# Two attention blocks on one core: the softmax sums of a turn fetched by two transfers of two rows, and another seed for the planner

## The chip, the cores and the metric

The kernel runs on one core of a Trainium2 chip. The metric is the time of one execution in microseconds on the device; the time of a version is the median of several runs. A separate execution is taken with the hardware profiler, and all lines of a profile come from that one execution. The engines are named as in the profile: PE (TensorE, matmuls), ACT (ScalarE, activations), DVE (VectorE), POOL (GpSimd) and SP (SyncE, which here only issues transfers). A transfer (DMA) issued by SP goes through SP's own in-order queue: an issue that has to wait holds those behind it.

## The reference

Input `x` has 2048 tokens of 1024 features in bf16; there are 32 heads of 32 features. Four residual blocks follow each other, A, B, A, B, each on a layer-normalised input:

- Block A is linear attention. With `q`, `k`, `v = x @ wqkv`, both `q` and `k` are mapped to `concat(softmax(w_phi q), softmax(-w_phi q))` per head; then `kv = sum_s phi_k v`, `z = sum_s phi_k`, and `o = (phi_q kv) / (phi_q z + 1e-6)`.
- Block B is full softmax attention: `p = softmax(q k^T / sqrt(32))`, `o = p v`.

Each ends with `x = x + o @ wo`. The change touches block B alone: the division of the weighted values by the sums of the softmax.

## The kernel before

The program is built in two rounds ("layers" in the code); a round is a block A and a block B. Tokens are cut into 4 chunks of 512, features into 8 groups of 128 (4 heads each). `xT` holds the residual stream transposed and stays in SBUF.

Every piece of work is first declared as an operation with an engine, a guessed duration, dependencies, buffers and a due number (`prio`). `Sched.run` (from line 170) then plays a list scheduler in the building program: on every engine it takes the ready operation with the smallest due number for which buffers are free, and the order in which operations are taken is the order in which the instructions are written. [...] Buffers are limited by class (`QUOTA`, line 329: four of `T`, two of `cden`, two of `den`, and so on), so the guessed times also set when buffers are thought to come free.

Two details of the scheduler belong to the change. First, at the head of `run` every planned duration of a DVE or PE operation is multiplied by a random factor between 0.99 and 1.01, drawn in order of declaration from a generator seeded with `TIE` (line 56). Transfers take no draw. The factors alter the plan, not the instructions themselves:

```
draw = random.Random(TIE)
for o in self.ops:
    if TIE and o.eng in ("DVE", "PE"):
        o.dur *= 1 + draw.uniform(-0.01, 0.01)
```

Second, a transfer is declared by `dma` (line 520) with 0.55 us of issue time on its queue and a latency of `2.0 + kb / 200` us, to which `slack` is added; `kb` also lengthens a common model of the transfer engines (`ring`) by `kb / 400` us.

Block B is `attention` (line 1211). It runs over turns, pairs of a query chunk `qc` and a head group `g`; there are 32 turns in a round. A turn has two halves `pp` of two heads each. For every unit of 128 keys and one head PE computes scores (line 1257) into PSUM; ACT exponentiates two or three units at once (line 1273), and some units go to DVE instead, with a polynomial of five instructions (lines 1184 to 1203). PE then multiplies the exponentials with the values and with ones (line 1305), so the accumulator of a half holds, in one 64-partition half, the weighted values of two heads, and in the other half their sums, each sum repeated over 32 partitions. Which half is which alternates with `pp`. In the gaps PE does "filler" work of the same round or of the next one: projections of keys, queries and values, output projections, and in the first round the key side of the next block A.

When a half is done, DVE copies the accumulator to an SBUF tile `T` (line 1321). When both are, a turn is finished as follows (lines 1351 to 1373):

1. The four sum rows of the turn's four heads, 512 float32 each, are fetched by transfers on SP's queue out of the two `T` tiles and spread over the 128 partitions of `cden`: 32 partitions of 16 numbers for each head (line 1354). The transfers out of a `T` tile need only that tile's copy.
2. DVE takes the reciprocal of `cden`, 128 x 16 (line 1361).
3. SP writes it to a DRAM scratch tensor `rd`, 8 KB (line 1362), and fetches it back with each head's row repeated over 32 partitions, 128 x 512 float32, into `den` (line 1364).
4. DVE multiplies the two `T` tiles with it (line 1370) and leaves the turn's output in bf16 for the output projection.

The last turn of a round divides in another way (lines 1328 to 1349), so 62 of the 64 turns do this. SP's queue also carries the pieces of the keys (line 1049), the swapped halves of the queries (lines 1070 and 1071), queries put away and fetched back in the first round (lines 1083, 1091 to 1093) and the stores of the result (line 1172). Loads of weights in the attention go over POOL's queue (lines 705 and 709).

Of the kernel before, what the change touches and what calls it, by code (L numbers as in the profile page):

```python
# [52 lines left out]
OVER = {"DVE": 0.085, "ACT": 0.012}  # L53
NEXT = {"DVE": 0.05, "ACT": 0.13}
RING = 0.5
TIE = 17
LOOK = 8


# [10 lines left out]
class Sched:  # L70
# [11 lines left out]
    def op(self, eng, dur, fn, deps=(), bufs=(), prio=0.0, lat=None, mode=None):  # L82
        o = Op(eng, dur, LAT[eng] if lat is None else lat, fn, tuple(bufs), prio, mode, len(self.ops))
        for d in deps:
            if d is not None:
                d.out.append(o)
                o.ndep += 1
        for b in o.bufs:
            b.left += 1
        if eng == "DVE" and any(b.kind == "ps" and b.banks in ([(7,)], [(6,)]) for b in o.bufs):  # L90
            o.ahead = EVAC
        self.ops.append(o)
        return o
# [76 lines left out]
    def run(self):  # L170
# [4 lines that stand above are left out]
# [201 lines left out]
def kernel(  # L376
# [11 lines left out]
    nc = tc.nc  # L388
# [47 lines left out]
    for j in range(4):  # L436
# [4 lines left out]
        out=rep[:].rearrange("p (x j) -> p x j", j=4),  # L441
        in_=J_bf[:].rearrange("p (j d) -> p d j", d=32)[:, 0:8, :],
    )
    nc.vector.tensor_copy(out=fold[:], in_=ident[:, 0:32])
    for a in range(1, 4):
        nc.vector.tensor_tensor(
            out=fold[:], in0=fold[:], in1=ident[:, 32 * a:32 * a + 32], op=ALU.add
# [4 lines left out]
        out=selb[:].rearrange("p (j d) -> p j d", d=32),  # L452
        in_=pick[:].unsqueeze(2).to_broadcast([P, 4, 32]),
# [32 lines left out]
    def sb(cls, *dims, dt=BF16):  # L486
        n = 1
        for d in dims:
            n *= d
        b = Buf("sb", -(-n * (4 if dt == F32 else 2) // 64) * 64, cls)  # L490
        b.with_ = ()

        def v():
            ap = arena[:, b.at // 2:b.at // 2 + n * (2 if dt == F32 else 1)]
            if dt == F32:
                ap = ap.bitcast(F32)
            if len(dims) == 2:
                ap = ap.rearrange("p (a b) -> p a b", a=dims[0])
            elif len(dims) == 3:
                ap = ap.rearrange("p (a b c) -> p a b c", a=dims[0], b=dims[1])  # L500
            return ap

        return b, v
# [16 lines left out]
    def dma(prio, fn, deps=(), bufs=(), q="SP", kb=256, issue=0.55):  # L520
        return op(q, issue, fn, deps, bufs, prio, lat=2.0 + kb / 200.0)
# [202 lines left out]
    def phi():  # L724
        return phi_t[:].rearrange("p (g n) -> p g n", g=G)
# [485 lines left out]
    def attention(base, kT, vT, q_of, gate, extra):  # L1211


        def when(u):
            return base + 10 * pos[(u[0], u[1])] + 5 * u[2] + 0.5 * u[3]
# [12 lines left out]
        while units:  # L1228
# [17 lines left out]
            prio = front = max(front, when(grp[0]))  # L1246
# [19 lines left out]
            if own is not None:  # L1266
# [7 lines left out]
                out=e_v(), in_=s_v()[:, 0:w * C512], func=ACT.Exp, scale=math.log(2) / BITS),  # L1274
# [6 lines left out]
        if True:  # L1281
            for qc, g in turns:
                T = []
                end = (qc, g) == turns[-1]
                for pp in range(2):
# [5 lines left out]
                    for n, (d, u) in enumerate(order):  # L1291
                        prio = base + 10 * pos[(qc, g)] + 5 * pp + 0.5 * (n // 2)
# [31 lines left out]
                prio = base + 10 * pos[(qc, g)] + 12  # L1324
# [3 lines left out]
                if end:  # L1328
# [3 lines left out]
                        out=r_v()[hi_, b * P:(b + 1) * P], in_=T[0][1]()[hi_, b * P:(b + 1) * P]),  # L1332
                        [T[0][2]], [d_b, T[0][0]], prio) for b in range(4)]
                    s = [op("DVE", dve_us(512), lambda o_v=o_v, r_v=r_v, T=T: nc.vector.tensor_tensor(
                        out=o_v()[lo_, :], in0=T[0][1]()[lo_, :], in1=r_v()[hi_, :], op=ALU.mult),
# [3 lines left out]
                    for ns in (slice(0, 256), slice(256, 512)):  # L1339
                        ln = op("ACT", act_us(256), lambda ns=ns, l_v=l_v, a_v=a_v: nc.scalar.activation(  # L1340
                            out=l_v()[lo_, ns], in_=a_v()[lo_, ns], func=ACT.Ln), [last], [a_b, l_b], prio)
                        ln = op("ACT", act_us(256), lambda ns=ns, l_v=l_v: nc.scalar.activation(
                            out=l_v()[lo_, ns], in_=l_v()[lo_, ns], func=ACT.Exp, scale=-1.0), [ln], [l_b], prio)
                        cut.append(s + [op("DVE", dve_us(256), lambda ns=ns, o_v=o_v, l_v=l_v, a_v=a_v: nc.vector.tensor_tensor(
                            out=o_v()[hi_, ns], in0=a_v()[hi_, ns], in1=l_v()[lo_, ns], op=ALU.mult),
# [5 lines left out]
                c_b, c_v = sb("cden", 16, dt=F32)  # L1351
                at_d = rd_v[len(gone)]
                gone.append((qc, g))
                m = [dma(prio, lambda k=k, i=i, c_v=c_v, T=T: nc.sync.dma_start(
                    out=c_v()[64 * k + 32 * i:64 * k + 32 * i + 32, :],
                    in_=T[k][1]()[64 * (1 - k) + 32 * i:64 * (1 - k) + 32 * i + 1, :].rearrange(
                        "r (s c) -> r s c", c=16)),
                    [T[k][2]], [c_b, T[k][0]], kb=2) for k in range(2) for i in range(2)]
                for o in m:
                    o.slack = 1.5  # L1360
                rc = op("DVE", 0.245, lambda c_v=c_v: nc.vector.reciprocal(out=c_v(), in_=c_v()), m, [c_b], prio)
# [1 line left out]
                    out=at_d.rearrange("h (s c) -> (h s) c", c=16), in_=c_v()), [rc], [c_b], kb=8)  # L1363
                bk = dma(prio, lambda r_v=r_v, at_d=at_d: nc.sync.dma_start(
                    out=r_v(), in_=at_d.unsqueeze(1).to_broadcast([4, 32, C512])), [aw], [d_b], kb=600)
# [3 lines left out]
                for k, a in ((1, slice(0, P)), (0, lo_)):  # L1369
                    s.append(op("DVE", dve_us(512), lambda a=a, k=k, o_v=o_v, r_v=r_v, T=T: nc.vector.tensor_tensor(  # L1370
                        out=o_v()[a, :], in0=T[k][1]()[a, :], in1=r_v()[a, :], op=ALU.mult),
# [9 lines left out]
        out=phi()[32 * j:32 * j + 32, :, 32 * j:32 * j + 32],  # L1381
        in_=A_w_phi.rearrange("(g j) i f -> j i g f", j=4)[j]), (), (), q="GQ", kb=16) for j in range(4)]
# [14 lines left out]
    for layer in range(2):  # L1397
# [29 lines left out]
        else:  # L1427
            wq_s = [slab("slab", second - 15 + fc, wdq_v[:, :, fc * C512:(fc + 1) * C512], C512, [store["q"][fc]])
                    for fc in range(2)]
            for c in range(NC - 1):  # L1430
                x_b, x_v = sb("xn", PO, C512)
                xnA[c] = (x_b, x_v, [dma(second - 20 + 20 * c + 0.001 * i, lambda c=c, x_v=x_v, i=i: nc.gpsimd.dma_start(
                    out=x_v()[:, 2 * i:2 * i + 2, :], in_=xd_v[:, c, 2 * i:2 * i + 2, :]),
# [53 lines left out]
        if wide == NC:  # L1487
            for i in range(pos[(2, HALF)], len(turns)):
                qc, g = turns[i]
                pl = at + 10 * i - LATE  # L1490
                wl = slab("w2", pl - 3, B_w[:, :, g * P:(g + 1) * P], P, [q_of[turns[i - 2]][2][0]])
                q_of[(qc, g)] = b_q(g, qc, pl, wl, FIL)
        oTs, last_s = attention(at, kT, vT, q_of, gate, lambda i: PAIRS[COUNT[layer][i]])
        if last:
            bo_s = [slab("slab", at + BO + fc, B_o[:, :, fc * C512:(fc + 1) * C512], C512, [q_of[(1, G - 1)][2][0]])
# [42 lines left out]
        if not last:  # L1538

            kv = new_kv()  # L1540
            for c, p0 in AK:
# [4 lines left out]
                    out=xd_v[:, c, 2 * i:2 * i + 2, :], in_=xv()[:, 2 * i:2 * i + 2, :]), [fin[i]], [xb], q="GQ", kb=256)  # L1546
# [46 lines left out]
```

## Time and profile before

| | us |
|---|---|
| runs, median of 3 | 2245.67 (2244.37 to 2248.56) |
| profiled execution | 2247.36 |
| its span, first to last instruction | 2245.1 |
| PE busy in the span | 2176.1 |
| ACT busy | 1985.7 |
| DVE busy | 1855.9 |
| POOL busy | 197.0 |
| line 1273, exponentials on ACT, 1366 instructions | 1668.5 |
| line 1361, reciprocals on DVE, 62 instructions | 15.0 |
| line 1370, multiplies on DVE, 124 instructions | 83.9 |

How to read the lines: `L1273` is line 1273 of the kernel; `arena` is the one large SBUF tile in which the scheduler places nearly all buffers, so most names in a line are `arena`, `psum` or a DRAM tensor. `out<-in` gives what an instruction writes and reads. A row of the busy shares has 40 digits, one for each fortieth of the span, in tenths. A row of a table by stretches of time gives, for each engine, busy microseconds and in brackets the number of instructions, then the clock granted to PE, the share of the DMA engines' time and the rate in GB/s. A row of waits gives who waited, for what, total microseconds, how often, and the longest. A row in order of time gives the start, the duration, engine and line, the operation, and in square brackets the idle time before it with what ended it; `SPq` is an issue on SP's queue, whose duration is that of issuing, not that of the data's way. Consecutive instructions of one line are merged (`x2`). A row for a line of the source gives minimum, median and maximum duration in ns, and the first and last start.

PE and ACT instructions overlap a little with their neighbours, so a busy share near 100% is not yet a full engine.

### The profile page before, as it was taken

The page shows a single profiled execution, that of the slowest core. Times are in us where ns is not written, and L with a number is a line of the kernel's source. Part 1 is how long each engine was busy: PE and PEld are TensorE (multiplying, and loading weights), DVE is VectorE, ACT ScalarE, POOL GpSimd, SP SyncE. Part 2 cuts the span into 40 slices and gives each one's busy share as a digit, 9 for nine tenths or more (in the row PEclk, how much of TensorE's full clock was granted, in tenths as well). Part 3 has the DMA queues.
Part 4 walks back from the last instruction along what each step waited for, and adds up shares of the span by engine and source line. Part 5 has one row for each costly group of instructions (what it writes and reads, how often), then busy time and mean ns, then how long its engine had stood idle before and what let it go on. Part 6 is the DMA issues. An engine that isn't in the chain of part 4 may idle for free.

```text
span 2245.1 us, 82636 instructions
## 1 busy us (share of the span) xinstructions
PE 2176.1 (97%) x36788; PEld 872.2 (39%) x36788; DVE 1855.9 (83%) x2761; ACT 1985.7 (88%) x1939; POOL 197.0 (9%) x299
## 2 busy tenths in 40 slices
PE   7999999999999999999999999999999999999999
PEld 4554454444333333333333444433333333333333
DVE  7986873698899889677887788799999999988968
ACT  4436669999999999999998555999999999999998
POOL 1110000000001010121124200000000000100000
PEclk9999999999999999999999999999999999999999
DMA  9220101111122221222235100111111100211111
GB/s 207 49 81 3 33 24 42 41 34 34 51 57 88 74 73 54 64 96 73 78 110 152 59 5 10 36 37 38 36 29 29 35 24 19 73 31 35 47 36 38
DMA packets 121789, 119.67 MB, mean 53 GB/s; under 512 B 57752, under 2 KB 99800, under 8 KB 121432
## 3 DMA queue, kind: packets, MB, share of 16 engines
q1 hardware_dynamic: 102392, 56.64, 10.0%
q0 software_dynamic: 17424, 56.18, 8.7%
q8 instruction: 287, 4.70, 0.9%
q10 hardware_dynamic: 1616, 1.57, 0.2%
q14 instruction: 70, 0.57, 0.1%
HBM read 79.23 MB, written 14.14 MB: 42 GB/s over the span
## 4 chain that ended last, share of the span: by engine, by line
PE 28%; ACT 23%; DVE 9%; issue 5%; DMA 1%; SPq 0%; ACTq 0%; DVEq 0%
ACT arena L1273 22%; PE psum L530 14%; PE psum L1305 6%; PE psum L1257 6%; DVE arena L1203 2%; DVE arena L1184 1%; DVE arena L1196 1%; DVE arena L1201 1%; DVE arena L1193 1%; ACT arena L823 1%; DMA arena<-arena 1%; DVE arena L1370 1%; DVE arena L1198 1%; DVE arena L1057 1%; PE psum L994 0%
## 5 line engine op out<-in xcount | busy, mean ns | idle before, releaser
L1273 ACT ACTIVATE arena<-psum 128x1536 bf16<-128x1536 f32 (+1 forms) x1366 | 1668.5, 1446 | 12.0 <-PE psum L1257 7.1
L530 PE MATMUL psum<-arena 128*32 128x512 bf16 (+1 forms) x18432 | 1058.3, 358 | 12.5 <-DVE arena L836 2.7
L530 PEld LDWEIGHTS <-arena 128*32 128x32 bf16 x18944 | 459.8, 96 | 447.2 <-issue 175.7
L1305 PE MATMUL psum<-arena 128*32 128x512 bf16 x4096 | 628.1, 383 | 4.0 <-issue 2.0
L1305 PE MATMUL psum<-arena,ones_bf 128*32 128x512 bf16 x4096 | 628.1, 383 | 0.0
L1257 PE MATMUL psum<-arena 32*128 32x512 bf16 x4096 | 536.2, 383 | 27.2 <-ACT arena L1273 22.4
L1257 PEld LDWEIGHTS <-arena 32*128 32x128 bf16 x4096 | 158.4, 91 | 555.8 <-issue 549.0
L1184 DVE TENSOR_SCALAR arena<-psum 128x512 int32<-128x512 f32 x418 | 284.5, 686 | 101.7 <-PE psum L1257 90.3
L1203 DVE SCALAR_TENSOR_TENSOR arena<-arena 128x1024 int16<-128x1024 int32 x209 | 254.7, 1218 | 5.7 <-DVE arena L1201 0.4
L1305 PEld LDWEIGHTS <-arena 128*32 128x32 bf16 x4096 | 163.2, 95 | 227.8 <-issue 177.0
L1305 PEld LDWEIGHTS <-ones_bf 128*32 128x32 bf16 x4096 | 161.3, 95 | 22.3 <-issue 7.9
L705 POOL DMA_DIRECT2D arena<-in_B_wqkv_dram x46 | 42.2, 919 | 1248.6 <-PE psum L530 302.5
L1193 DVE TENSOR_SCALAR arena<-arena 128x1024 f16<-128x1024 int16 x209 | 143.8, 690 | 4.4 <-DMA arena<-arena 0.3
L1196 DVE TENSOR_TENSOR arena<-arena 128x1024 f16<-128x1024 f16 x209 | 142.6, 684 | 4.6
L1201 DVE TENSOR_TENSOR arena<-arena 128x1024 f16<-128x1024 f16 x209 | 142.6, 684 | 3.1
L1057 DVE CAST arena<-psum 128x512 bf16<-128x512 f32 x128 | 87.7, 685 | 57.6 <-PE psum L530 57.3
L823 ACT ACTIVATE arena<-psum 128x512 bf16<-128x512 f32 x80 | 43.0, 596 | 82.6 <-PE psum L530 66.7
L827 DVE TENSOR_REDUCE arena<-arena 128x32 f32<-128x1024 bf16 x64 | 77.0, 1214 | 33.3 <-ACT arena L823 33.2
L530 PE MATMUL psum<-xT,onesD 128*32 128x512 bf16 x1144 | 103.1, 381 | 1.3 <-DVE arena L836 0.7
L1321 DVE COPY arena<-psum 128x512 f32<-128x512 f32 x126 | 86.3, 685 | 15.4 <-PE psum L1305 15.0
L1198 DVE TENSOR_SCALAR arena<-arena 128x1024 f16<-128x1024 f16 x209 | 87.9, 422 | 1.7
L836 DVE TENSOR_TENSOR arena<-psum,arena 128x1024 bf16<-128x1024 f32 x64 | 77.4, 1219 | 13.3 <-PE psum L530 9.7
(124 smaller groups left out, 1383.6 us busy)
## 6 DMA issues: line engine op xcount, KB each, us to landing
arena<-rd SPq DMA_DIRECT2D x62, 256.0 KB
arena<-in_B_wqkv_dram POOLq DMA_DIRECT2D x58, 256.0 KB, 4.1
arena<-in_B_wo_dram POOLq DMA_DIRECT2D x40, 256.0 KB, 4.4
arena<-arena SPq DMA_DIRECT2D x256, 32.0 KB
arena<-wd_k POOLq DMA_DIRECT2D x32, 256.0 KB, 5.0
arena<-in_A_wqkv_dram POOLq DMA_DIRECT2D x32, 256.0 KB, 4.6
arena<-arena SPq DMA_DIRECT2D x96, 64.0 KB
arena<-arena SPq DMA_DIRECT2D x248, 2.0 KB
```

The source lines that it names most:

```text
L530: nc.tensor.matmul(out_[ks, :], lhsT=lhsT[:, ks], rhs=rhs, start=start, stop=stop, tile_position=(0, 32 * k), skip_group_check=True)
L1057: return op("DVE", dve_us(512), lambda: nc.vector.tensor_copy(out=dst(), in_=src()), [dep], bufs, prio)
L1184: o = op("DVE", dve_us(512), lambda: nc.vector.tensor_scalar(out=x_v()[:, k, :].bitcast(I32), in0=s_v()[:, x * C512:(x + 1) * C512], scala ...
L1193: last = op("DVE", 1024 / 1920 + 0.15, lambda: nc.vector.tensor_scalar(out=z(), in0=x_v().bitcast(I16).rearrange("p a (n two) -> p a n two ...
L1196: last = op("DVE", 1024 / 1920 + 0.15, lambda: nc.vector.tensor_tensor(out=u(), in0=z(), in1=z(), op=ALU.mult), [last], [z_b, u_b], prio + ...
L1198: last = op("DVE", 1024 / 3840 + 0.15, lambda: nc.vector.tensor_scalar(out=u(), in0=u(), scalar1=POW2_C[0], scalar2=POW2_C[1], op0=ALU.mul ...
L1201: last = op("DVE", 1024 / 1920 + 0.15, lambda: nc.vector.tensor_tensor(out=u(), in0=z(), in1=u(), op=ALU.mult), [last], [z_b, u_b], prio + ...
L1203: return op("DVE", dve_us(1024), lambda: nc.vector.scalar_tensor_tensor(out=y_v().bitcast(I16), in0=x_v().bitcast(I32), scalar=128.0 / BIT ...
L1257: nc.tensor.matmul(out=s_v()[:, x * C512:(x + 1) * C512], lhsT=kT[g][1]()[r, pp, d * P:(d + 1) * P], rhs=q_of[(qc, g)][1]()[r, (pp + j // ...
L1273: ex = op("ACT", act_us(w * C512), lambda s_v=s_v, e_v=e_v, w=w: nc.scalar.activation(out=e_v(), in_=s_v()[:, 0:w * C512], func=ACT.Exp, s ...
L1305: nc.tensor.matmul(out=a_v()[col:col + 32, :], lhsT=v_v()[:, kc % 4, o:o + DH] if what == 0 else ones_bf[:], rhs=ev()[:, x * C512:(x + 1) ...
L1321: cp = op("DVE", dve_us(512), lambda t_v=t_v, a_v=a_v: nc.vector.tensor_copy(out=t_v(), in_=a_v()), [last], [a_b, t_b], prio - 4)
```

## The change

Line 1354 declared four transfers for a turn: for each `T` tile `k` and each head `i` of it, one row of 512 numbers into 32 partitions. Now there are two: for each `T` tile one transfer whose source is the two rows 32 partitions apart, and whose target is 64 partitions. The declared size is 4 KB instead of 2 for each. The reciprocal depends on two transfers instead of four. The slack of 1.5 us is the same. Besides, the seed `TIE` goes from 17 to 19.

```
-TIE = 17
+TIE = 19
...
-                m = [dma(prio, lambda k=k, i=i, c_v=c_v, T=T: nc.sync.dma_start(
-                    out=c_v()[64 * k + 32 * i:64 * k + 32 * i + 32, :],
-                    in_=T[k][1]()[64 * (1 - k) + 32 * i:64 * (1 - k) + 32 * i + 1, :].rearrange(
+                m = [dma(prio, lambda k=k, c_v=c_v, T=T: nc.sync.dma_start(
+                    out=c_v()[64 * k:64 * k + 64, :],
+                    in_=T[k][1]()[64 * (1 - k):64 * (1 - k) + 33:32, :].rearrange(
                         "r (s c) -> r s c", c=16)),
-                    [T[k][2]], [c_b, T[k][0]], kb=2) for k in range(2) for i in range(2)]
+                    [T[k][2]], [c_b, T[k][0]], kb=4) for k in range(2)]
```

## The prediction

> **What bounds the kernel now.** I read the page first (span, busy shares, the chain that ended last), then the busy time by stage, then the waits of each engine and of the DMA queue, and last the instructions of single turns in order of time. From the page:
>
> ```profile
> span 2245.1 us, 82636 instructions
> PE 2176.1 (97%) x36788; PEld 872.2 (39%) x36788; DVE 1855.9 (83%) x2761; ACT 1985.7 (88%) x1939; POOL 197.0 (9%) x299
> ...
> ACT  4436669999999999999998555999999999999998
> ...
> PE 28%; ACT 23%; DVE 9%; issue 5%; DMA 1%; SPq 0%; ACTq 0%; DVEq 0%
> ACT arena L1273 22%; PE psum L530 14%; PE psum L1305 6%; PE psum L1257 6%; DVE arena L1203 2%; DVE arena L1184 1%; DVE arena L1196 1%; DVE arena L1201 1%; DVE arena L1193 1%; ACT arena L823 1%; DMA arena<-arena 1%; DVE arena L1370 1%; DVE arena L1198 1%; DVE arena L1057 1%; PE psum L994 0%
> ```
>
> The ACT row shows two long runs of nines: the attention of the first and of the second round. There the exponentials of line 1273 hold the chain; outside them it is TensorE. DMA is 1% of the chain, SyncE's queue 0%. I cut the span at the edges of those runs:
>
> ```profile
> core 0: us, PE busy (x) PEld busy (x) DVE busy (x) ACT busy (x) POOL busy (x), PEclk, DMA share, GB/s
> 0.00:327.00 327.00, 306.55 (x6839) 163.46 (x6843) 263.27 (x367) 172.01 (x291) 31.35 (x66) 1.00 0.30 67
> 327.00:1187.00 860.00, 838.02 (x13337) 309.10 (x13330) 675.21 (x997) 851.50 (x726) 109.82 (x153) 1.00 0.23 65
> 1187.00:1440.00 253.00, 248.71 (x4788) 117.92 (x4776) 196.72 (x277) 167.34 (x254) 34.46 (x56) 0.99 0.19 52
> 1440.00:2235.00 795.00, 776.76 (x11711) 278.64 (x11709) 716.28 (x1114) 792.50 (x665) 21.38 (x25) 1.00 0.13 35
> ```
>
> In the first attention ScalarE is idle 860.0 - 851.5 = 8.5 us, in the second 795.0 - 792.5 = 2.5 us. Between them TensorE is idle 253.0 - 248.7 = 4.3 us. These are what a better order could win; for what a worse one could lose the rows give no such limit.
>
> **The change, part by part.** It edits two things: the transfers of line 1354, and the seed TIE. One turn's path through line 1354 on SyncE's queue and VectorE:
>
> ```profile
> 1014.22 1.17 SPq L1354 DMA_DIRECT2D arena<-arena  x2
> 1019.77 0.33 SPq L1362 DMA_DIRECT2D rd<-arena  x1
> 1022.16 0.58 SPq L1364 DMA_DIRECT2D arena<-rd  x1
> ```
>
> ```profile
> 1019.49 0.25 DVE L1361 RECIPROCAL arena<-arena 128x16 f32<-128x16 f32 x1
> ...
> 1031.83 0.68 DVE L1370 TENSOR_TENSOR arena<-arena 128x512 bf16<-128x512 f32 x1
> ```
>
> The second pair of one-row transfers goes out at 1014.22, the reciprocal starts at 1019.49, its result goes to DRAM at 1019.77 and is fetched back at 1022.16, and the first multiply starts at 1031.83, among other VectorE work. The queue holds nothing between these times; it waits.
>
> *Transfers removed.* The queue's row for line 1354:
>
> ```profile
> L1354 SPq DMA_DIRECT2D arena<-arena x248: 502/582/1520, 349.1 to 2215.2; - x124
> ```
>
> 248 one-row issues are 62 turns x 4. The change leaves 124, so at 0.582 us each SyncE's queue is free of 124 x 0.582 = 72 us, if an issue of two rows costs what one of one row does; if it costs what two cost (1.17 us, above) nothing is freed. The bytes are the same. What this frees on the path is bounded by what waits for DMA:
>
> ```profile
> DVE arena L1065 <- DMA arena<-rd: 3.2, 1, 3.2
> DVE arena L1361 <- DMA qd<-arena: 1.0, 1, 1.0
> DVE arena L1370 <- DMA arena<-rd: 0.6, 1, 0.6
> DVE arena L1361 <- DMA arena<-arena: 0.5, 2, 0.3
> DVE arena L1193 <- DMA arena<-arena: 0.3, 1, 0.3
> ```
>
> ```profile
> SPq L1354 <- DVE arena L1321: 288.4, 85, 19.0
> ```
>
> VectorE waits for transfers 3.2 + 1.0 + 0.6 + 0.5 + 0.3 = 5.6 us in all (the wait for the input at the start apart), and the queue itself stands 288 us at line 1354 waiting for the copy of the sums. So the 72 us come out of slack. One place is different, early in the second attention, where the key transfers of line 1049 fill the queue:
>
> ```profile
> 1510.38 0.59 SPq L1364 DMA_DIRECT2D arena<-rd  x1
> ...
> 1512.88 1.23 SPq L1354 DMA_DIRECT2D arena<-arena  x2
> 1514.21 8.31 SPq L1049 DMA_DIRECT2D arena<-arena  x8
> ```
>
> ```profile
> 1510.38 7.76 DMA arena<-rd
> ```
>
> ```profile
> 1518.23 0.69 DVE L1370 TENSOR_TENSOR arena<-arena 128x512 bf16<-128x512 f32 x1 [0.59 <-DMA arena<-rd]
> ```
>
> Eight issues take 8.31 us there, over a microsecond each, and the fetch issued at 1510.38 lands only 7.76 us later. Fewer issues ahead of it are worth that 0.6 us. I take -0.6; the ends are 0 and -5.6.
>
> *Landing of a two-row transfer.* No row shows one. The reciprocal at line 1361 needs both transfers. In the planner each issue is 0.55 us, so the pair that closes a turn is promised 0.55 us sooner and the reciprocal's place in VectorE's order moves up by as much. Now it starts 1019.49 - 1014.22 = 5.3 us after the first issue of the pair; then it is some 4.7 us. It is queued on VectorE in order, so a late landing holds every VectorE instruction behind it, the evacuations of line 1184 among them, and through these ScalarE and TensorE. Against that, the 128-piece transfer of line 1362 lets its successor go 1022.16 - 1019.77 = 2.4 us after its own issue, landing included. So 2.3 us of margin remain. The ends are 0 and the case of a transfer that lands after 4.7 us (a rival below). Line 1361 now waits 1.0 + 0.5 = 1.5 us in 3 of 62 turns; with 0.55 us less margin I take as much again, +1.5.
>
> *Moved work.* The write-back of line 1362, the fetch of line 1364 and the two multiplies of line 1370 may each be placed up to about 0.55 us sooner. Between 1022.16 and 1031.83 lie 9.7 us, and the tiles T, cden and den have at least two buffers. I cost this at nothing; what covers it is that gap, and if it were gone the multiplies would hold VectorE as line 1361 does. SyncE's other work (key pieces, query swaps, stores) moves up in the queue at most by the 1.2 us that a turn saves. GpSimd's queue gets and loses no issue.
>
> *The other seed.* TIE sets the random factors of 0.99 to 1.01 on each planned VectorE and TensorE duration, which decide ties. Every factor changes, so the whole written order changes, from the start of the kernel on. No row prices this; the spread between stretches of the present order is the nearest:
>
> ```profile
> core 0: us, ACT busy (x), PEclk, DMA share, GB/s
> ...
> 700.00:800.00 100.00, 100.00 (x84) 1.00 0.28 79
> 800.00:900.00 100.00, 99.82 (x86) 1.00 0.22 61
> 900.00:1000.00 100.00, 97.03 (x86) 0.98 0.26 79
> 1000.00:1100.00 100.00, 99.25 (x88) 1.00 0.29 82
> 1100.00:1187.00 87.00, 83.92 (x77) 0.98 0.32 103
> ...
> 1800.00:1900.00 100.00, 100.00 (x86) 1.00 0.09 23
> 1900.00:2000.00 100.00, 100.00 (x86) 1.00 0.19 53
> ```
>
> Stretches lose between 0.0 and 3.1 us of ScalarE. In the stretches of 3.0 and 3.1 us TensorE's granted clock is 0.98 as well. The first attention loses 8.5 of 860, 0.99%; the second loses 2.5 of 795, 0.31%, although its VectorE is fuller (716.3 of 795 = 90%, against 675.2 of 860 = 79%). I see nothing in the second stage's work that would make it the smoother one, so I take it that this order happens to suit it, and give it the first one's rate: 0.99% x 795 = 7.9, less 2.5, +5.4 us. Ends: all idle time of ScalarE won, -11.0, and TensorE's middle idle with it, -4.3; on the other side the loss of 3.0 us in six more stretches of about 100 us, +18.
>
> *Sum.* -0.6 + 1.5 + 0 + 5.4 = +6.3 us on the profiled execution, which took 2247.36 us (span 2245.1 and 2.3 around it): 2253.7. The median of the three runs, 2245.67, is 1.7 below that execution, so the forecast for the median is 2252.0.
>
> **Rivals.** *Faster: the new order packs the first attention as this one packs the second.* Then 0.31% x 860 = 2.7 us of idle time are left of 8.5, -5.8; half of the 4.3 us in the middle, -2.1; and the queue's relief of 0.6 us, without any new wait at line 1361: -8.5, or 2237. For it speaks that 5.9 of the first stage's 8.5 us of idle time lie in two stretches of bad order (2.97 in 900 to 1000, 3.08 in 1100 to 1187), so two repairs do it. Against it, that the second stage must then keep its 2.5. It decides from the point at which the first stage's gain exceeds the second's loss.
>
> *No change: all of it hidden.* The queue's 72 us come out of waiting time, gains and losses of the order cancel between the stages: 2245, within 2. If the issue of two rows costs twice, so that the change doesn't shorten the queue at all, the result is the same.
>
> *Much slower: the two-row transfer is late.* The 64 pieces of 64 bytes may share few of the 16 DMA engines. What a piece costs an engine, from the page:
>
> ```profile
> q1 hardware_dynamic: 102392, 56.64, 10.0%
> ```
>
> 10.0% of 16 x 2245.1 us over 102392 packets is 0.035 us. On two engines 32 pieces take 1.1 us, so the landing comes at 2.4 + 1.1 = 3.5 us, inside the 4.7; on one engine 2.4 + 2.2 = 4.6, at the edge. It decides where 32 pieces take over 4.7 - 2.4 = 2.3 us, or 0.07 us each, or where the queue is as full as at 1514. At 1 us late per turn VectorE stands 62 us; in the second attention 31 us of that meet 79 us of free VectorE time, so I pass on a quarter of the 62, +15: 2261. The Trainium skill's page "DMA: Bandwidth & Descriptors", section "Why a DMA increments its semaphore by 16 and not by 1", gives a rule that speaks against the change: a transfer runs on the largest number of engines, up to 16, that divides the slowest dimension of both its sides. A one-row source has 32 pieces as that dimension, so 16 engines; a two-row source has 2, so two engines. By that rule the two-engine figure is the one that holds, and the landing slips but stays inside the margin. No trace here shows a two-row source.
>
> **How the numbers follow.** A measurement of this kernel tells some 0.2%, 4.5 us, from no change. The forecast, slower by 2 to 10 us mostly through the order, has 0.38; the late transfer 0.12; no change 0.22; the better-packed order 0.28. So faster 0.28, same 0.22, slower 0.50. The forecast's own range is 2248 to 2258. For 8 in 10 I go down to 2233 (past the faster rival's 2237 towards the 15 us of both idle sums) and up to 2266 (past the late transfer's 2261; +18 on the median would be 2264).
>
> **What would show it.** Right: 124 issues at line 1354 of about 0.58 us; waits at line 1361 of 2 to 4 us in all; ScalarE's idle time in the second attention near 8 us, in the first near 8; PE and DVE instruction counts the same but for idle fillers. Wrong: line 1361 waiting over 10 us (late transfer); a second attention still at 2 to 3 us of idle with a first under 5 (faster). The forecast fails above all if the idle rate of a stage is not a matter of the drawn order, or if the two stages outside the attentions move by more than the few microseconds I give them.

## The result, and the profile after

The changed kernel takes 2644.98 us (median of 4 runs, 2638.95 to 2646.85) against 2245.97 us (median of the 4 runs of before made with them): slower by a ratio of 1.178 (95% interval 1.176 to 1.180), some 400 us. The prediction said 2252, with 2266 as its upper end. The profiled execution took 2638.95 us.

The page of the changed kernel, with the rows that answer to those of before:

```profile
span 2636.7 us, 82489 instructions
PE 2289.1 (87%) x36784; PEld 883.5 (34%) x36784; DVE 1875.1 (71%) x2761; ACT 2014.9 (76%) x1939; POOL 197.6 (7%) x299
...
ACT  5356588878787878888876757777888788787887
...
q1 hardware_dynamic: 98672, 56.63, 8.5%
...
L1273 ACT ACTIVATE arena<-psum 128x1536 bf16<-128x1536 f32 (+1 forms) x1366 | 1694.4, 1344 | 372.6 <-DMA arena<-arena 276.4
```

The work is the same (2761 VectorE and 1939 ScalarE instructions in both), but the two runs of nines in ScalarE's row have become sevens and eights. The last row says why: the 1366 exponentials now have 372.6 us of idle time ahead of them. The same row of the page before reads

```profile
L1273 ACT ACTIVATE arena<-psum 128x1536 bf16<-128x1536 f32 (+1 forms) x1366 | 1668.5, 1446 | 12.0 <-PE psum L1257 7.1
```

The difference, 372.6 - 12.0 = 360.6 us, is nearly the whole growth of the span, 2636.7 - 2245.1 = 391.6 us. The largest releaser is a transfer, with 276.4 us.

Busy time by stage, cut at the edges of the exponentials' runs (columns as in the prediction):

```profile
core 0: us, PE busy (x) PEld busy (x) DVE busy (x) ACT busy (x) POOL busy (x), PEclk, DMA share, GB/s
0.00:327.00 327.00, 305.61 (x6804) 161.88 (x6808) 262.14 (x367) 170.25 (x288) 31.46 (x66) 1.00 0.30 67
327.00:1396.00 1069.00, 911.01 (x13606) 321.55 (x13595) 696.61 (x1016) 884.05 (x743) 120.58 (x166) 0.93 0.20 55
1396.00:1632.00 236.00, 228.77 (x4524) 109.64 (x4517) 182.37 (x255) 148.99 (x238) 24.89 (x42) 1.00 0.16 44
1632.00:2626.00 994.00, 837.35 (x11733) 285.42 (x11736) 729.50 (x1118) 809.28 (x667) 20.64 (x25) 0.92 0.10 28
```

The attentions grew from 860 to 1069 us and from 795 to 994 us, +209 and +199; the stretch between them went from 253 to 236, and the start is unchanged. So the loss lies where line 1354 runs, and in both rounds alike. Which transfers the exponentials wait for is told by the row of line 1354 and by who waited for it:

```profile
L1354 SPq DMA_DIRECT2D arena<-arena x124: 497/549/624, 351.2 to 2603.6; - x124
...
  ACT arena L1273: 276.4, 106
  POOL arena L705: 240.9, 10
...
  DVE arena L1057: 52.8, 19
...
  DVE arena L1193: 40.6, 25
  DVE arena L1370: 34.6, 12
  DVE arena L1203: 13.2, 6
```

The reciprocal of line 1361, which does need the sums, is not among the ten longest entries, of which seven are shown; its own row of waits for a transfer within `arena` is small:

```profile
DVE arena L1361 <- DMA arena<-arena: 4.6, 2, 2.4
```

Before, the list of line 1354 held the reciprocal, with 0.5 us, and two entries of GpSimd of some 15 us each. Save for the multiplies of line 1370, none of the instructions named here has any use for the sums: line 1273 writes exponentials, line 1057 keys and values, lines 1193 and 1203 are steps of the polynomial, line 705 loads weights. All they share with the transfer is that they write into `arena`. The transfers in turn wait for work that has nothing to do with them; the queue's own waits:

```profile
SPq L1354 <- DVE arena L1321: 180.1, 45, 18.3
...
SPq L1354 <- DMA arena<-in_B_wo_dram: 70.3, 12, 10.9
SPq L1354 <- DMA arena<-arena: 56.0, 35, 3.9
...
SPq L1354 <- ACT arena L1273: 44.3, 59, 2.0
SPq L1354 <- DMA arena<-wd_k: 44.0, 7, 16.6
```

The sums come from line 1321 alone; weight loads (`in_B_wo_dram`, `wd_k`) and exponentials don't touch them. Each transfer thus acts as a fence for much of what is written to the large tile. One such fence, in order of time:

```profile
608.09 2.84 ACT L1273 ACTIVATE arena<-psum 128x1536 bf16<-128x1536 f32 x2
613.23 1.02 ACT L1273 ACTIVATE arena<-psum 128x1024 bf16<-128x1024 f32 x1 [2.30 <-DMA arena<-arena]
```

```profile
611.30 0.56 SPq L1354 DMA_DIRECT2D arena<-arena  x1
```

```profile
611.68 0.69 DVE L1184 TENSOR_SCALAR arena<-psum 128x512 int32<-128x512 f32 x1 [0.41 <-PE psum L1257]
613.24 0.69 DVE L1193 TENSOR_SCALAR arena<-arena 128x1024 f16<-128x1024 int16 x1 [0.87 <-DMA arena<-arena]
```

```profile
614.30 0.52 PE L1257 MATMUL psum<-arena 32*128 32x512 bf16 x3 [2.23 <-ACT arena L1273]
```

The exponential ends at 608.09 + 2.84 = 610.93, the transfer goes out at 611.30, and 1.9 us later, at 613.23 and 613.24, ScalarE and VectorE go on at the same moment: it has landed. ScalarE stood 2.30 us, and TensorE, whose next scores wait for that exponential, 2.23 us. The fence does not hold every write to `arena`: line 1184, the first step of the polynomial, writes there too, yet it starts at 611.68, while the transfer is under way, and none of the idle time ahead of its 418 instructions ends with a transfer.

### The profile page after: what moved, and what is told of

Its sections match the earlier page's. It is cut to its first block, busy times and chain, and to the rows that moved or that the text cites. A ratio compares the mean times of both kernels' runs of the same rounds, so it can differ in the third digit from the quotient of the medians.

```text
span 2636.7 us, 82489 instructions
## 1 busy us (share of the span) xinstructions
PE 2289.1 (87%) x36784; PEld 883.5 (34%) x36784; DVE 1875.1 (71%) x2761; ACT 2014.9 (76%) x1939; POOL 197.6 (7%) x299
## 3 DMA queue, kind: packets, MB, share of 16 engines
q1 hardware_dynamic: 98672, 56.63, 8.5%
## 5 line engine op out<-in xcount | busy, mean ns | idle before, releaser
L1273 ACT ACTIVATE arena<-psum 128x1536 bf16<-128x1536 f32 (+1 forms) x1366 | 1694.4, 1344 | 372.6 <-DMA arena<-arena 276.4
L530 PE MATMUL psum<-arena 128*32 128x512 bf16 (+1 forms) x18432 | 1077.6, 363 | 19.0 <-DVE arena L1057 3.7
L1257 PE MATMUL psum<-arena 32*128 32x512 bf16 x4096 | 570.9, 408 | 299.9 <-ACT arena L1273 296.3
L1305 PE MATMUL psum<-arena 128*32 128x512 bf16 x4096 | 678.0, 410 | 2.0 <-DVE arena L1321 1.5
L1305 PE MATMUL psum<-arena,ones_bf 128*32 128x512 bf16 x4096 | 677.6, 410 | 0.7 <-issue 0.7
L530 PEld LDWEIGHTS <-arena 128*32 128x32 bf16 x18944 | 462.0, 97 | 468.5 <-issue 200.8
L1305 PEld LDWEIGHTS <-arena 128*32 128x32 bf16 x4096 | 168.5, 97 | 256.0 <-issue 207.2
L1305 PEld LDWEIGHTS <-ones_bf 128*32 128x32 bf16 x4096 | 166.8, 97 | 21.8 <-issue 6.8
L530 PE MATMUL psum<-xT,onesD 128*32 128x512 bf16 x1112 | 108.7, 414 | 0.8 <-DVE arena L836 0.7
L1370 DVE TENSOR_TENSOR arena<-arena 128x512 bf16<-128x512 f32 x124 | 84.3, 680 | 34.9 <-DMA arena<-arena 34.6
```

Source lines behind the costliest of these rows:

```text
L530: nc.tensor.matmul(out_[ks, :], lhsT=lhsT[:, ks], rhs=rhs, start=start, stop=stop, tile_position=(0, 32 * k), skip_group_check=True)
L1257: nc.tensor.matmul(out=s_v()[:, x * C512:(x + 1) * C512], lhsT=kT[g][1]()[r, pp, d * P:(d + 1) * P], rhs=q_of[(qc, g)][1]()[r, (pp + j // ...
L1273: ex = op("ACT", act_us(w * C512), lambda s_v=s_v, e_v=e_v, w=w: nc.scalar.activation(out=e_v(), in_=s_v()[:, 0:w * C512], func=ACT.Exp, s ...
L1305: nc.tensor.matmul(out=a_v()[col:col + 32, :], lhsT=v_v()[:, kc % 4, o:o + DH] if what == 0 else ones_bf[:], rhs=ev()[:, x * C512:(x + 1) ...
```

## The experiments

Three theories were on trial. A: false order, the program lets the two-row source wait for, and hold up, nearly everything written to the large tile. B: the two-row transfer itself lands late, since it runs on two DMA engines. C: the order drawn with seed 19 is bad.

The edits of E1 and E2 are shown against the kernel before, the others against the changed kernel; E3 and E7 also have `TIE` back at 17. Each ratio is to runs of the kernel before made in the same comparison: their median is 2244.61 us for E1 to E4, 2248.62 for E5 to E7 and 2244.66 for E8 to E11.

**The transfers alone (E1).** The change with seed 17.

```
 TIE = 17
...
-in_=T[k][1]()[64 * (1 - k) + 32 * i:64 * (1 - k) + 32 * i + 1, :]
+in_=T[k][1]()[64 * (1 - k):64 * (1 - k) + 33:32, :]
```

> Two transfers of two rows 32 partitions apart, with the seed of before (17). Theory A, false order: the program orders a source of two rows with a step between them against nearly everything in the one big tile, so exponentials and VectorE work wait for each of these transfers and they wait for earlier work; the seed hardly matters: 2600 to 2680 us, and line 1273 waits over 200 us for transfers of line 1354. Theory B, late landing on two DMA engines: the same time, but the waits stand at the reciprocal of line 1361. Theory C, the redrawn order of seed 19 costs the time: 2240 to 2260 us.

Measured: 2643.69 us, ratio 1.178 (1.176 to 1.180).

```profile
ACT arena L1273 <- DMA arena<-arena: 274.1, 111, 10.8
...
DVE arena L1361 <- DMA arena<-arena: 1.8, 2, 1.0
```

The first row is that of the exponentials, the second that of the reciprocal. The time is that of the change, so the seed is not the cause (C falls); and the waits stand at the exponentials, not at the reciprocal, which is against B.

**The seed alone (E2).**

```
-TIE = 17
+TIE = 19
```

> Four transfers of one row as before, with the seed 19. Theories A and B: within some 10 us of before, 2238 to 2260 us; this also prices the term of the prediction for the other seed, put at +5.4 us. Theory C: 2600 us or more.

Measured: 2249.21 us, ratio 1.0020 (1.0010 to 1.0029), +4.6 us: a small loss, clear of the noise.

**Adjacent rows (E3, E4).** Each sum stands in 32 partitions alike, so partitions 31 and 32 of a 64-partition half hold the same two heads as 0 and 32, without a step between them.

```
-in_=T[k][1]()[64 * (1 - k):64 * (1 - k) + 33:32, :]
+in_=T[k][1]()[64 * (1 - k) + 31:64 * (1 - k) + 33, :]
```

> Two transfers of two rows that lie next to each other (rows 31 and 32 of the 64, which hold the same sums of the two heads as rows 0 and 32), seed 17. The same bytes, pieces and number of issues as the change, and by the slowest dimension of the source the same two DMA engines. Theory A: no step between the rows, no false order, so 2240 to 2255 us and no wait of line 1273 for line 1354. Theory B: as slow as the change, 2600 us or more.

> The changed kernel with one thing undone, the step between the two rows (rows 31 and 32 in place of 0 and 32); seed 19. Theory A: 2240 to 2260 us, near the run with four one-row transfers and seed 19. Theory B: 2600 us or more. The difference to that run prices the two issues saved in a turn alone: -5 to +3 us.

Measured: 2257.04 us with seed 17, ratio 1.0061 (1.0044 to 1.0077); 2244.28 us with seed 19, ratio 1.0008 (0.9998 to 1.0018), no change that can be told. The run with seed 19 differs from the changed kernel in these two rows only, and it wins back the 400 us. From its page, its queue's rows for line 1354, and its waits:

```profile
q1 hardware_dynamic: 98672, 56.63, 9.9%
...
L1273 ACT ACTIVATE arena<-psum 128x1536 bf16<-128x1536 f32 (+1 forms) x1366 | 1669.4, 1425 | 8.3 <-PE psum L1257 5.8
```

```profile
L1354 SPq DMA_DIRECT2D arena<-arena x124: 512/578/680, 349.3 to 2211.7; - x124
L1354 SPq EVENT_SEMAPHORE  x105: 17/17/11759, 347.1 to 2199.9; - x105
```

```profile
SPq L1354 <- ACT arena L1273: 1.1, 3, 0.6
...
DVE arena L1361 <- DMA arena<-arena: 1.7, 1, 1.7
```

The same 98672 packets as in the changed kernel, the same 124 issues, of 0.58 us, and the idle time of the exponentials is 8.3 us. The first row of the waits has fallen from 44.3 to 1.1 us, and the reciprocal waits once. B falls.

The second row of line 1354 counts the semaphore instructions with which the queue waits for other engines and transfers ahead of these issues (columns as for the issues; the longest here stood 11.8 us). In the changed kernel that row reads

```profile
L1354 SPq EVENT_SEMAPHORE  x265: 17/28/15173, 348.2 to 2589.6; - x133
```

These are instructions of the program. For the same 124 transfers it holds 265 of them with the step and 105 without, as many as for the 248 transfers of before. So the additional waits of the transfers are written into the program as built; they do not arise on the chip.

With seed 17 the same edit missed its expected range, 2240 to 2255 us, by 2 us at the upper end; that is taken up under the other seeds.

**Only the second round (E6).**

```
+in_=(T[k][1]()[64 * (1 - k):64 * (1 - k) + 33:32, :] if layer else
+     T[k][1]()[64 * (1 - k) + 31:64 * (1 - k) + 33, :])
```

> Rows 32 partitions apart in the second round only, adjacent rows in the first; seed 19. Theory A: each transfer with a step costs by itself, so 62 of the 124 transfers cost about half of the 400 us: 2420 to 2470 us, with the first attention as long as before (about 860 us) and the second some 200 us longer. If the loss came from one place, or from an order that fails as a whole: near 2245 or near 2645 us.

Measured: 2444.45 us, ratio 1.0876 (1.0858 to 1.0894), half of the loss (2248.62 before, in the same comparison: +196 us).

```profile
327.00:1187.00 860.00, 839.03 (x13442) 308.74 (x13438) 679.38 (x1003) 854.70 (x732) 111.19 (x153) 1.00 0.23 65
1187.00:1442.00 255.00, 245.55 (x4743) 115.59 (x4740) 192.99 (x272) 164.93 (x251) 34.64 (x56) 0.99 0.19 51
1442.00:2431.00 989.00, 831.82 (x11730) 284.92 (x11726) 728.36 (x1116) 806.90 (x666) 20.80 (x25) 0.93 0.10 28
```

The first attention runs as before, the second needs 989 us in place of 795. The loss follows the transfers with a step, 196 / 62 = 3.2 us for each.

**A step of two (E7).** Rows 30 and 32, seed 17.

```
-in_=T[k][1]()[64 * (1 - k):64 * (1 - k) + 33:32, :]
+in_=T[k][1]()[64 * (1 - k) + 30:64 * (1 - k) + 33:2, :]
```

> Two rows two partitions apart (rows 30 and 32 of the 64), seed 17. Theory A in its strict form, any step between the rows brings the false order: 2600 to 2680 us. If the distance of 32 partitions matters, because the order covers only the partitions between the rows: still slow wherever a write touches these partitions, and nearly all writes touch all 128, so the same. If only a distance over some size matters: 2240 to 2260 us.

Measured: 2695.68 us, ratio 1.200 (1.197 to 1.203). The smallest step brings the false order too, 16 us beyond the expected range. It costs 2695.68 - 2643.69 = 52 us more than the step of 32 with the same seed. The idle time of the exponentials grew by nearly as much, from 369.3 us in E1 to 420.1; why they lose more to this step isn't shown.

**T in a tile of its own (E5), and its control (E8).** The rows of the change, 32 apart, but the four `T` buffers out of `arena`; it has to shrink by their 8 KB in each partition. The control has adjacent rows.

```
-SBUF_ARENA = 172 * 1024 - 256
+SBUF_ARENA = 164 * 1024 - 256
...
+own_t = const.tile([P, 4 * C512], F32, tag="own_t")
+own_n = []
...
-t_b, t_v = sb("T", C512, dt=F32)
+t_b = Buf("sb", 64, "T")
+own_n.append(0)
+t_v = lambda at_=(len(own_n) - 1) % 4: own_t[:, at_ * C512:(at_ + 1) * C512]
```

> The changed kernel with its rows 32 partitions apart, but the four T buffers lie in a tile of their own, and the big tile is 8 KB smaller by that. The transfers are those of the change: same rows, same step, same pieces, same number. Theory A, false order inside the big tile: 2240 to 2265 us, and no wait of line 1273 for the transfers. If instead the step between the rows is slow on the chip itself: 2600 us or more.

> The kernel with T in a tile of its own and the big tile 8 KB smaller, but with adjacent rows. If the 82 us that the own tile with rows 32 apart still stands over before come from the smaller big tile and the plan that it forces: the same time, 2325 to 2336 us. If a step between the rows costs something even in a tile of its own: 2240 to 2300 us.

Measured: 2330.60 us, ratio 1.0366 (1.0350 to 1.0381), with the step, and 2329.86 us, ratio 1.0371 (1.0352 to 1.0389), without. The first missed its range of 2240 to 2265; its control says why. Out of the large tile the step costs nothing that can be told, and what is left over before belongs to the smaller `arena` and the plan made for it, which both runs share. In the run with the step (the exponentials are line 1275 there):

```profile
L1275 ACT ACTIVATE arena<-psum 128x1536 bf16<-128x1536 f32 (+1 forms) x1366 | 1666.1, 1439 | 5.7 <-PE psum L1259 2.0
...
L1358 SPq EVENT_SEMAPHORE  x100: 17/17/10120, 350.3 to 2285.7; - x100
...
L822 DVE COPY arena<-psum x24: 678/691/693, 891.0 to 1273.3; 128x512 f32<-128x512 f32 x24
```

The exponentials have 5.7 us of idle time and none behind a transfer, and the transfers (line 1358 there) have 100 waits of the queue ahead of them, with the very rows that had 265 in the large tile. The last row is the copy of the next block A's keys, which is filler of the first attention: its last one starts at 1273.3, where it started at 1170.1 before. The plan with less room finishes that filler after the attention has ended, with ScalarE mostly idle.

**Other seeds (E9, E10, E11).** Adjacent rows with `TIE` 5, 7 and 11.

> Adjacent rows with another seed, 5, to see how far a redrawn order alone moves the time: between 2238 and 2262 us by the runs so far (2244 for seed 19, 2257 for seed 17). A time below 2238 would beat both kernels.

> Adjacent rows with seed 7, for the same purpose as the run with seed 5: between 2238 and 2262 us; below 2238 it would beat both kernels.

> Adjacent rows with seed 11, for the same purpose as the run with seed 5: between 2238 and 2262 us; below 2238 it would beat both kernels.

Measured: 2249.84 us, ratio 1.0025 (1.0015 to 1.0034); 2254.59 us, 1.0038 (1.0024 to 1.0051); 2283.58 us, 1.0164 (1.0146 to 1.0182). With 2244.28 for seed 19 and 2257.04 for seed 17 five seeds of one and the same program text spread over 39 us, and none is faster than the kernel before by more than the noise. Seeds 5 and 7 fall in their expected range of 2238 to 2262 us; seed 11 misses it by 22 us. It shows the same sign as the smaller `arena`, its copies of keys reaching to 1223.7:

```profile
L820 DVE COPY arena<-psum x24: 673/684/692, 883.7 to 1223.7; 128x512 f32<-128x512 f32 x24
```

That this late filler makes its 39 us is read from the row and wasn't tested by a run.

What is shown, then: the 400 us come from a step between the rows of the source while it lies in the large tile; they vanish with the step, and with the tile. That the waits are built into the program is shown by their count, 265 against 105 and 100. That its ordering takes such a source for a range over a large part of the tile is inferred from who waits for whom; line 1184 shows that it isn't all of it, and the exact range stays open. Which step in building the program adds the waits was not tested.

## Why the prediction was wrong

- **What bounds the kernel** was right: ScalarE's exponentials held the attentions, which is why fences of about 2 us on them come through undiminished, and with some loss besides (the last section).
- **The step that failed is the landing of a two-row transfer.** The prediction took it that only the reciprocal of line 1361 waits for the transfer, and put the term at +1.5 us, with a late landing as its far end (+15). The reciprocal hardly waits at all (4.6 us in the changed kernel, 1.8 in E1, 1.7 in E4). What wait are the writers of the tile that holds the source: 276 us at the exponentials, in a loss of 400. The part asked how long the transfer takes, and not what else the program orders against its operands once their shape changes. No row of the trace of before shows a source with a step, so its cost could not be read there; but a rival "the new shape brings new waits" was missing, and with it all of the loss.
- **Moved work at nothing** failed by the same omission: it reckoned with a transfer moving within its old waits, while the queue now waited 59 times at line 1354 for exponentials, 44.3 us in all, where E4 has 3 such waits.
- **Transfers removed**: 124 issues of 0.55 us (0.58 in E4), as said. Their worth can't be told from the redrawn order: at seed 19 two transfers beat four by 2249.21 - 2244.28 = 4.9 us, at seed 17 they lose 2257.04 - 2244.61 = 12.4 us. The forecast of -0.6 is neither borne out nor refuted.
- **The other seed**, +5.4 us: 4.6 us alone (E2). The size came out by luck, for the route was another. The two attentions of E2, over the stretches used in the prediction, are

```profile
327.00:1187.00 860.00, 836.13 (x13347) 306.65 (x13339) 677.04 (x1001) 853.76 (x728) 112.86 (x153) 1.00 0.22 65
...
1440.00:2235.00 795.00, 773.07 (x11689) 275.79 (x11689) 713.75 (x1111) 790.51 (x662) 20.99 (x25) 1.00 0.13 35
```

The second one's ScalarE idles 795.0 - 790.5 = 4.5 us and not the 7.9 forecast, and the first one's 860.0 - 853.8 = 6.2 in place of 8.5: together 0.3 us less idle time than before, where 5.4 more were forecast. And the upper end of +18 was short: seed 11, with adjacent rows, shows +39 us, by a route that the prediction didn't list.
- **A slip in the rival of the better-packed order**: the two stretches of bad order add up to 2.97 + 3.08 = 6.1 us and not 5.9; nothing else hangs on it.
- **The rival of the late transfer.** Its condition, two engines, holds. Queue q1 has 102392 - 98672 = 3720 packets less. The pieces of data are as many as before (248 x 32 = 124 x 64). If each engine in use adds one closing packet, 248 transfers on 16 engines less 124 on two make 248 x 16 - 124 x 2 = 3720 exactly. Both the number of engines and a closing write by each of them are stated by the Trainium skill's page "DMA: Bandwidth & Descriptors", section "Why a DMA increments its semaphore by 16 and not by 1", and these packet counts agree with it. The price was wrong: the transfer followed above lands within 1.9 us of its issue, against the 3.5 us estimated, and in E4, with the same two engines, nothing is lost.

## What to carry to other kernels

When an access changes its shape, ask first what the program will now order against it, and only then what the transfer costs: here, in a large tile that holds many buffers, a source that stepped over partitions turned each transfer into a fence. The sign in the profile is a wait for a transfer at an instruction that has no use for its data. Where a value stands in several partitions, choose adjacent ones; and where a planner breaks ties by a seed, price an edit over several seeds before believing a few microseconds.

## What the runs showed of the hardware

TensorE's granted clock can give way after a pause of little more than 2 us. Around the fence shown above, in the changed kernel (columns as in the tables by stage),

```profile
609.00:612.00 3.00, 3.00 (x46) 0.94 (x41) 1.71 (x3) 1.93 (x2) 0.00 (x0) 1.00 0.12 42
612.00:614.00 2.00, 0.08 (x4) 0.09 (x1) 1.06 (x2) 0.77 (x1) 0.00 (x0) 1.00 0.02 2
614.00:617.00 3.00, 2.70 (x22) 0.63 (x25) 1.55 (x3) 2.22 (x4) 0.00 (x0) 0.57 0.00 0
```

a pause of 2.23 us is followed by 3 us at a granted clock of 0.57. A pause of that length doesn't always do it; later in the same run one of 2.29 us is followed by 3 us at the full clock:

```profile
2001.52 0.40 PE L1257 MATMUL psum<-arena 32*128 32x512 bf16 x3 [2.29 <-ACT arena L1273]
```

```profile
2001.50:2004.50 3.00, 2.98 (x57) 1.33 (x60) 2.73 (x6) 3.00 (x3) 0.00 (x0) 1.00 0.02 5
```

So a fence can cost TensorE again after it has ended: over the attentions the clock averages 0.93 and 0.92 where it was 1.00. The exponentials wait 276 / 124 = 2.2 us per transfer directly, of the 3.2 us that each costs. Besides, they wait 76.6 us for the scores of line 1257, against 7.1 before. How much of that the lower clock makes wasn't separated.
